# A clustered-attention, dense and routed-expert kernel: first pair's clusters and the passage to the dense layer in a new order, second products of 128-slot experts in rounded parts, 128 slots for the first expert

## The chip, the cores and the metric

One core of one Trainium2 chip runs the kernel. The metric is the device time of one execution in microseconds (us). Before the change three runs gave 716.62, 715.57 and 715.26 us, median 715.57.

## The reference, cut to what matters

Three layers follow each other: attention whose mask keeps a query and a key only if both chose the same of 16 centroids; a dense layer with an ELU between two products; and routed experts for the tokens whose skip score is positive.

```python
# attention: batch 2, heads 8, tokens 768, head size 64, 16 centroids per head
q_assign = argmax(einsum('bhsd,hcd->bhsc', q_n, c_n)); k_assign = argmax(einsum('bhsd,hcd->bhsc', k_n, c_n))
scores = where(q_assign == k_assign, (q @ k.T) / sqrt(D), -1e9)
x = softmax(scores) @ v                                # 1536 tokens x 512
# dense: w_in 512 x 2048, w_out 2048 x 512
h = x @ w_in;  g = where(h > 0, h, exp(min(h, 0)) - 1);  x = g @ w_out
# experts: 8 of them, w1 512 x 1024, w2 1024 x 512
xc = x[x @ w_skip > 0];  e_idx = argmax(xc @ w_gate);  gate = max of softmax(xc @ w_gate)
out[those] = xc + gate * (maximum(xc @ w1[e], 0) @ w2[e])      # e is the token's expert
```

## The kernel before, in words

**Attention.** The 16 (batch, head) blocks are done as 8 pairs of two heads. For a pair, q, k and v are loaded as `natq`, `natk`, `natv` (`load_nat`, L213). TensorE turns them (`turn`, L239) into PSUM; ACT rounds them to the high part `qH`, `kH` (`turn_head`, L247), and a subtraction gives the low part `qL`, `kL` (`turn_rest`: DVE for the first pair, POOL for the others, L259 and L261). Products of rounded values, three per product (high by high, low by high, high by low), then make the similarity to the centroids (`similar`, L280, 6 matmuls per 384 tokens). The clusters are chosen in a row of steps: turn back (L289), copy (L295), largest `mx` (L302), difference (L306), candidates (L311), first `mn` (L316), one-hot `oh` (L320), turn of the one-hot (L326), and the mask rows on ACT (L330). SP's queue moves q, k parts and mask rows into the operands `QA`, `KA`, `QB`, `KB` of each head (`move_qk`, `move_mask`). Then, in chunks of 128 queries: scores (L375), peak (L381, DVE), exponent (L388, ACT, tile `pe`), turning (flip, L397), high part `ptH` (L409, ACT), low part `ptL` (L415, DVE), product with the values (L428).

**Order.** Attention and the beginning of the dense layer are issued in an order written out by hand. `SCHEDULE` is a list of step names; `+` and `-` in front of a name mean the step of the next or the last pair. `attention` walks it once for each pair. Before the change the first `AHEAD = 20` steps of the second pair were issued ahead with the first pair's. In the last pair the names `W0` to `W6` stand for the dense layer's first products.

**Dense.** Weights are given in a form that is first rounded on the device to 32 bits of their own (`round_half`): ACT makes `cv_a` and `cv_t` (L644, L646), DVE makes `cv_a` again and `cv_b` in two steps (L648, L650, L653), POOL makes `r` (L655); ACT then takes `w1H` (L674) and POOL `w1L` (L675). The first two chunks' weights come from the generator `early_weights`, advanced by `next(self.early)` at places of the order and drained at the end of attention. `ffn_h` (L688) multiplies a chunk of 128 hidden columns for 384 tokens, 12 matmuls; `ffn_elu` is `e`, `e` on ACT, one DVE step into PSUM, `gH` on ACT, `gL` on DVE (L703 to L709); L720 is the second product. 32 rounds cover two halves of the tokens by 16 chunks.

**Experts.** Expert 0 is fixed as the first, the others are ranked by their count; each has so many slots as `WIDTHS` says (160, 160, 144, 128 five times). For the first expert the tokens of the second batch are picked by matmuls with a selection (`first_x`, L935), while a gathered tile gives those of the first batch. `expert` (L1086) runs 8 steps f of 128 hidden columns: first product of 4 matmuls (L1113), ReLU to `h` on ACT (L1115), second product one step later. With more than 128 slots ("not direct") the weights stand still and `h` moves, 4 matmuls per f with columns as wide as the slots (L1105), and the result `yT` is turned at the end (L1135). With 128 slots ("direct") `h` stands still and 512 columns of w2 move (L1102). All these are plain f32. `expert_load` fetches half an expert's w1 and w2, 1 MiB each, on SP's queue.

Of the kernel before, what the change touches and what calls it, by code (L numbers as in the profile page):

```python
# [27 lines left out]
WIDTHS = (160, 160, 144, 128, 128, 128, 128, 128)  # L28
# [10 lines left out]
AHEAD = 20  # L39
SCALE = {"q": 0.125, "k": 1.0}  # L40

LEAST_HI = struct.unpack("<f", struct.pack("<I", 897 << 20))[0]

# [17 lines left out]
class _Core:  # L61
# [24 lines left out]
    def centroids(self):  # L86
# [4 lines left out]
        nc.sync.dma_start(out=cn[:, 0, :], in_=self.cent.rearrange("h c d -> (h c) d"))  # L91
        self.load_nat(0, "qkv")
        self.zero = c.tile([128, 1], F32, name="zero")
        V.memset(self.zero, 0.0)
        S.activation(self.zero, self.zero, AF.Sqrt)
# [6 lines left out]
        t = c.tile([128, 8], F32, name="cnt")  # L102
# [4 lines left out]
        S.activation(self.zero, self.zero, AF.Exp)  # L107
# [105 lines left out]
    def load_nat(self, n, names):  # L213
        if n >= self.B * self.H // 2:
            return
        b, p = divmod(n, self.H // 2)
        for nm in names:
            src = {"q": self.q, "k": self.k, "v": self.v}[nm]
            shape = [128, 2, self.NC, 64] if nm == "v" else [128, self.NC, 2, 64]
            t = self.pre.tile(shape, F32, tag="nat" + nm, name="nat" + nm)  # L220
            for h in range(2):
                self.nc.sync.dma_start(out=t[:, h] if nm == "v" else t[:, :, h],
                                       in_=src[b, 2 * p + h].rearrange("(p c) d -> p c d", c=self.NC))
            self.nat[nm] = t
# [61 lines left out]
    def turn_back(self, n):  # L286
        ps = self.back[n] = self.bank_p()
        for c in range(self.NC):
            self.nc.tensor.transpose(ps[:, c * 64:c * 64 + 64], self.rows[0:64, c * 128:c * 128 + 128], self.ident[0:64, 0:64])  # L289

    def similarities(self, n):
        NG = self.NC * 4
        t = self.best[n] = {nm: self.pre.tile([128, NG] + [16] * w, dt, tag=nm, name=nm)
                            for nm, w, dt in (("eq", 1, F32), ("mx", 0, F32), ("mn", 0, F32), ("oh", 1, BF16))}
        self.nc.scalar.activation(t["eq"], self.back[n][:, 0:NG * 16].rearrange("p (g c) -> p g c", c=16), AF.Copy)  # L295

    def wide16(self, x):
        return x.unsqueeze(2).to_broadcast([128, self.NC * 4, 16])

    def largest(self, n):  # L300
        t = self.best[n]
        self.nc.vector.tensor_reduce(t["mx"], t["eq"], axis=AX.X, op=ALU.max)  # L302

    def less_largest(self, n):
        t = self.best[n]
        (self.nc.gpsimd if n else self.nc.vector).tensor_tensor(t["eq"], t["eq"], self.wide16(t["mx"]), ALU.subtract)  # L306

    def candidates(self, n):

        t = self.best[n]  # L310
        self.nc.vector.scalar_tensor_tensor(t["eq"], t["eq"], 0.0, self.iota_neg.unsqueeze(1).to_broadcast([128, self.NC * 4, 16]),  # L311
                                            ALU.is_equal, ALU.mult)

    def first_of_them(self, n):
        t = self.best[n]
        self.nc.vector.tensor_reduce(t["mn"], t["eq"], axis=AX.X, op=ALU.min)  # L316

    def one_hot(self, n):
        t = self.best[n]
        self.nc.vector.tensor_tensor(t["oh"], t["eq"], self.wide16(t["mn"]), ALU.is_equal)  # L320

    def turn_one_hot(self, n):
        oh, ps = self.best.pop(n)["oh"], self.bank_p()
        pb = self.rows_ps[n] = ps[0:64, :].bitcast(BF16)
        for c in range(self.NC):
            self.nc.tensor.transpose(pb[:, c * 128:c * 128 + 128],  # L326
                                     oh[:, 4 * c:4 * c + 4, :].rearrange("p g c -> p (g c)"), self.ident16)

    def mask_rows(self, n):
        self.nc.scalar.activation(self.rows[64:128].bitcast(F32R), self.rows_ps.pop(n)[:, 0:self.S], AF.Identity,  # L330
                                  scale=self.oh_sc[:, 0:1], bias=self.oh_sc[:, 1:2])

    def move(self, o, i):
        self.nc.sync.dma_start(out=o.bitcast(F32), in_=i.bitcast(F32))
# [13 lines left out]
    def move_mask(self, n, s):  # L348
        d, o = self.hd[s], self.rows[64:128]
        self.move(d["QB"][64:80], o[16 * s:16 * s + 16])  # L350
        self.move(d["KB"][64:80], o[32 + 16 * s:48 + 16 * s])
# [135 lines left out]
    def steps(self):  # L487
# [9 lines left out]
        for h in range(2):  # L497
            for nm in "qk":
                for x, f in (("turn", self.turn), ("TH", self.turn_head), ("raw", self.turn_raw), ("TL", self.turn_rest),
                             ("sim", self.similar)):  # L500
                    put(at, f"{x}{nm}{h}", f, nm, h)
            put(at, f"sT{h}", self.similar_out, h)
# [36 lines left out]
    def attention(self):  # L539
# [12 lines left out]
        order = []  # L552
        for m in range(-3, NPAIR + 3):
            for what in SCHEDULE:
                name = what.lstrip("+-")
                n = m + what.count("+") - what.count("-")
                if 0 <= n < NPAIR and name not in (end if n == NPAIR - 1 else last):
                    order.append((m, n, name))

        first = [x for x in order if x[1] == 1][:AHEAD]  # L560
        first = [x for x in order if x[0] < 0 or x in first]
        self.prep_tags = itertools.cycle(("p", "v", "t0", "t1"))
        for m, n, name in first:
            steps[name](n)
        self.prep_tags = itertools.repeat("p")
        for m, n, name in order:
            if (m, n, name) not in first:
                steps[name](n)
# [333 lines left out]
    def first_fetch(self):  # L902
# [9 lines left out]
        self.pick = d.tile([SLOT, 2, CAP], F32, name="pick")  # L912
        V.memset(self.pick, 0.0)
        self.early = []
        for g, n in enumerate((SLOT, CAP - SLOT)):
# [415 lines left out]
```

## Time and profile before

| what | value |
|---|---|
| median of 3 runs | 715.57 us (715.26 to 716.62) |
| profiled execution, its own time | 716.21 us |
| its span | 714.4 us |
| mean granted TensorE clock | 0.983 of full |
| busy share: PE, DVE, ACT, POOL | 95%, 62%, 59%, 38% |

The span is the time from the first to the last recorded instruction; 1.8 us of the profiled execution lie around it. A busy share is an average over stages. Attention takes the span up to about 259 us, the dense layer up to about 575 us with the routing in its tail, and the experts the rest. PE marks TensorE's matmuls, PEclk the share of full clock that it was granted.

### The profile page before, as it was taken

The page shows a single profiled execution, that of the slowest core. Times are in us where ns is not written, and L with a number is a line of the kernel's source. Part 1 is how long each engine was busy: PE and PEld are TensorE (multiplying, and loading weights), DVE is VectorE, ACT ScalarE, POOL GpSimd, SP SyncE. Part 2 cuts the span into 40 slices and gives each one's busy share as a digit, 9 for nine tenths or more (in the row PEclk, how much of TensorE's full clock was granted, in tenths as well). Part 3 has the DMA queues.
Part 4 walks back from the last instruction along what each step waited for, and adds up shares of the span by engine and source line. Part 5 has one row for each costly group of instructions (what it writes and reads, how often), then busy time and mean ns, then how long its engine had stood idle before and what let it go on. Part 6 is the DMA issues. An engine that isn't in the chain of part 4 may idle for free. (4 is left out here: it accounts for less than half of the span.)

```text
span 714.4 us, 12083 instructions
## 1 busy us (share of the span) xinstructions
PE 680.5 (95%) x4288; PEld 609.5 (85%) x4288; DVE 444.7 (62%) x836; ACT 422.3 (59%) x924; POOL 268.9 (38%) x257
## 2 busy tenths in 40 slices
PE   4899999999999987999999999999999999999994
PEld 3699999999999876888888899999998989987773
DVE  5499999999989987999999732522633521110100
ACT  4699989999898976677666655445444111111110
POOL 0423536444465043666888633322322032110010
PEclk9799999999999999999999999999999999999998
DMA  7646657366644613555555374151102278898830
GB/s 179 144 90 146 147 136 161 99 146 150 156 100 103 175 46 132 183 196 183 178 176 177 119 285 186 60 177 60 59 30 77 120 264 306 264 319 306 293 107 12
DMA packets 73829, 111.54 MB, mean 156 GB/s; under 512 B 31169, under 2 KB 41505, under 8 KB 73760
## 3 DMA queue, kind: packets, MB, share of 16 engines
q1 hardware_dynamic: 72176, 106.55, 50.5%
q0 software_dynamic: 1584, 4.13, 1.6%
q8 instruction: 36, 0.59, 0.4%
q14 instruction: 33, 0.27, 0.1%
HBM read 73.94 MB, written 16.99 MB: 127 GB/s over the span
## 5 line engine op out<-in xcount | busy, mean ns | idle before, releaser
L415 DVE TENSOR_TENSOR ptL<-ps_t,ptH 128x384 fp32r<-128x384 f32 x192 | 102.7, 551 | 12.2 <-ACT ptH L409 9.9
L409 ACT ACTIVATE ptH<-ps_t 128x384 fp32r<-128x384 f32 x192 | 91.4, 489 | 17.8 <-PE ps_t L397 13.7
L397 PE MATMUL ps_t<-ident,pe 128*128 128x128 f32 x576 | 94.4, 277 | 3.3 <-DVE ptL L415 2.6
L428 PE MATMUL ps_v<-ptH,vt 128*128 128x256 f32 x288 | 78.3, 296 | 0.7 <-DVE xr L445 0.7
L397 PEld LDWEIGHTS ps_t<-ident,pe 128*128 128x128 f32 x576 | 68.2, 141 | 11.7 <-DVE ptL L415 7.4
L428 PE MATMUL ps_v<-ptL,vt 128*128 128x256 f32 x288 | 77.1, 296 | 0.0
L675 POOL TENSOR_TENSOR w2L<-r,w2H 128x512 fp32r<-128x512 f32 x28 | 42.4, 1515 | 69.6 <-PE ps_t L720 62.3
L655 POOL TENSOR_TENSOR r<-cv_b,cv_t 128x512 int32<-128x512 int32 x32 | 43.1, 1346 | 46.3 <-DVE cv_b L653 26.4
L428 PEld LDWEIGHTS ps_v<-ptH,vt 128*128 128x128 f32 x288 | 54.0, 190 | 2.7 <-DVE xr L445 1.3
L428 PEld LDWEIGHTS ps_v<-ptL,vt 128*128 128x128 f32 x288 | 53.5, 190 | 0.0
L381 DVE TENSOR_REDUCE st<-ps_sA 128x1 f32<-128x768 f32 x48 | 45.6, 950 | 11.4 <-PE ps_sA L375 11.2
L1139 POOL DMA_INDIRECT out_dram<-o,dest x11 | 10.8, 980 | 105.2 <-DVE o L1137 104.3
L703 ACT ACTIVATE e<-ps_p 128x384 f32<-128x384 f32 x32 | 15.7, 490 | 58.6 <-PE ps_p L688 58.6
L648 DVE SCALAR_TENSOR_TENSOR cv_a<-cv_a,d 128x512 f32<-128x512 f32 x32 | 45.6, 1425 | 5.4 <-ACT cv_a L644 5.1
L381 DVE TENSOR_REDUCE st<-ps_sB 128x1 f32<-128x768 f32 x48 | 45.7, 952 | 2.8 <-PE ps_sB L375 2.7
L688 PE MATMUL ps_p<-xH,w1H 128*128 128x384 f32 x128 | 44.0, 344 | 3.1 <-ACT w1H L674 3.1
L675 POOL TENSOR_TENSOR w1L<-r,w1H 128x512 fp32r<-128x512 f32 x32 | 44.1, 1379 | 7.1 <-ACT w1H L674 7.1
L388 ACT ACTIVATE pe<-ps_sA,st 128x768 f32<-128x768 f32 x48 | 43.4, 904 | 0.1
L706 DVE SCALAR_TENSOR_TENSOR ps_p<-e,ps_p 128x384 f32<-128x384 f32 x32 | 17.9, 559 | 40.9 <-ACT e L704 40.9
L388 ACT ACTIVATE pe<-ps_sB,st 128x768 f32<-128x768 f32 x48 | 43.0, 896 | 0.5 <-DVE st L381 0.3
L688 PE MATMUL ps_p<-xL,w1H 128*128 128x384 f32 x128 | 43.1, 336 | 0.0
L1115 ACT ACTIVATE h<-ps_v 128x128 f32<-128x128 f32 (+2 forms) x32 | 9.1, 285 | 56.1 <-PE ps_v L1113 47.1
(362 smaller groups left out, 1883.0 us busy)
## 6 DMA issues: line engine op xcount, KB each, us to landing
ew<-in_moe_w_dram SPq DMA_DIRECT2D x32, 1024.0 KB
d<-in_moe_w_in_dram SPq DMA_DIRECT2D x16, 512.0 KB
d<-in_moe_w_out_dram SPq DMA_DIRECT2D x16, 512.0 KB
wf_d<-r SPq DMA_DIRECT2D x16, 512.0 KB
r<-wf_d SPq DMA_DIRECT2D x16, 512.0 KB
KA<-kH SPq DMA_DIRECT2D x32, 192.0 KB
natq<-in_q_dram SPq DMA_DIRECT2D x16, 192.0 KB
natk<-in_k_dram SPq DMA_DIRECT2D x16, 192.0 KB
```

The lines of the kernel that those rows point to most:

```text
L381: self.nc.vector.tensor_reduce(st, self.sc[u][:, :, 0:384], axis=AX.XY, op=ALU.max, negate=True)
L388: self.nc.scalar.activation(pe, self.sc.pop(u)[:, :, 0:384], AF.Exp, bias=self.peaks.pop(u), accum_out=self.sums[n][:, s:s + 1])
L397: self.nc.tensor.transpose(ps[:, 0, j * 128:j * 128 + 128], self.pe[u][:, half, j * 128:j * 128 + 128], self.ident)
L409: self.nc.scalar.activation(self.split(u, half)[0], self.tp[u, half][:, 0, 0:384].rearrange("p (c q) -> p c q", c=3), AF.Copy)
L415: self.nc.vector.tensor_tensor(l, self.tp.pop((u, half))[:, 0, 0:384].rearrange("p (c q) -> p c q", c=3), h.bitcast(F32), ALU.subtract)
L428: self.nc.tensor.matmul(self.vp[n, j], lhsT=self.vt[n][:, j // NG, c, :], rhs=t, start=(part == 0 and i == 0), stop=(part == 3 and i == 2 ...
L648: V.scalar_tensor_tensor(a, a, LEAST_HI, hi.bitcast(F32), ALU.is_ge, ALU.mult)
L655: G.tensor_tensor(out.bitcast(I32), b, t, ALU.add)
L675: self.nc.gpsimd.tensor_tensor(l, x, h.bitcast(F32), ALU.subtract)
L688: self.nc.tensor.matmul(ps, lhsT=w[:, c, :], rhs=x[:, c, :], start=(i == 0), stop=(i == 11))
L703: S.activation(e, ps, AF.Relu, scale=-1.0)
L706: V.scalar_tensor_tensor(ps, e, -1.0, ps, ALU.add, ALU.max)
```

## The change

It has four parts.

- **Start.** The first pair's q is loaded first, centroids and k from ACT's queue, v from SP's. A list `START` replaces `AHEAD`. The first pair's choice of clusters is made in two halves of 192 columns, read straight from PSUM, without ACT's copy; half of the masks of keys moves on ACT's queue; scores of the first pair are issued before the second pair's similarities.
- **Passage.** The generator of early weights has five single steps for the first chunk, and `W0` to `W3` (`first_h`) each advance it once more.
- **First expert.** `WIDTHS[0]` is 128, not 160: it becomes a direct expert, and its selection matmuls have 128 columns and one group.
- **Second products of 128-slot experts.** `h` and w2 are split into rounded high and low parts (`hH`, `hL`; `ew2H`, `ew2L` or both in `ew2HL`), and three products of rounded values replace the f32 product. ACT makes the high parts, DVE the low ones, w2's two steps f ahead (`w2_split`).

```diff
-WIDTHS = (160, 160, 144, 128, 128, 128, 128, 128)
+WIDTHS = (128, 160, 144, 128, 128, 128, 128, 128)
...
+START = """
+    turnq0 THq0 turnq1 TLq0 THq1 turnk0 TLq1 THk0 turnk1 TLk0 THk1 TLk1 simq0 simk0 loadqk sT0 simq1 simk1 back0 mx0 sT1
...
-        nc.sync.dma_start(out=cn[:, 0, :], in_=self.cent.rearrange("h c d -> (h c) d"))
-        self.load_nat(0, "qkv")
...
+        self.load_nat(0, "q")
+        nc.scalar.dma_start(out=cn[:, 0, :], in_=self.cent.rearrange("h c d -> (h c) d"))
+        self.load_nat(0, "k", nc.scalar)
+        self.load_nat(0, "v")
...
+    def largest(self, n, half=None):
+        t, g = self.best[n], self.groups_of(half)
+        self.nc.vector.tensor_reduce(t["mx"][:, g], (t["eq"] if n else self.back_groups(n))[:, g], axis=AX.X, op=ALU.max)
...
+        self.move(d["KB"][64:80], o[32 + 16 * s:48 + 16 * s], None if n or s else self.nc.scalar)
...
-            put(last, f"W{i}", lambda n, i: self.ffn_h(0, 0, 3 * i, 3 * i + 3), i)
+            put(last, f"W{i}", self.first_h, i)
...
+    def first_h(self, n, i):
+
+        self.ffn_h(0, 0, 3 * i, 3 * i + 3)
+        next(self.early, None)
...
-            for n in (2, 1, 1, 1):
+            for n in ((2, 1, 1, 1) if k else (1, 1, 1, 1, 1)):
...
+    def w2_split(self, e, f):
+
+        if e == self.E or WIDTHS[e] > SLOT:
+            return
+        j, i = divmod(f, self.F2 // 256)
+        w2 = self.ew[e, j][1][:, i, :]
+
+        if f % 2:
+            h, l = (self.fw.tile([128, 512], F32R, tag="w1" + x, bufs=2, name="ew2" + x) for x in "HL")
+        else:
+            hl = self.fw.tile([128, 2, 512], F32R, tag="r", bufs=3, name="ew2HL")
+            h, l = hl[:, 0], hl[:, 1]
+        self.nc.scalar.activation(h, w2, AF.Copy)
+        self.nc.vector.tensor_tensor(l, w2, h.bitcast(F32), ALU.subtract)
+        self.e2[e, f] = h, l
...
-                PE.matmul(y[0][0:W], lhsT=h, rhs=w2, start=(f == 0), stop=(f == NF - 1))
+                (hH, hL), (wH, wL) = h, w2
+                for i, (a, b) in enumerate(((hH, wH), (hL, wH), (hH, wL))):
+                    PE.matmul(y[0][0:W], lhsT=a, rhs=b, start=(f == 0 and i == 0), stop=(f == NF - 1 and i == 2))
...
-            S.activation(h, ps[:, 0:W], AF.Relu)
+            if direct:
+                hH, hL = h = [d.tile([128, SLOT], F32R, tag="h" + x, bufs=3, name="h" + x)[:, 0:W] for x in "HL"]
+                S.activation(hH, ps[:, 0:W], AF.Relu)
+                V.scalar_tensor_tensor(hL, ps[:, 0:W], 0.0, hH.bitcast(F32), ALU.max, ALU.subtract)
```

TensorE's order at the start, from the last of the second pair's turned keys (`natk`) on. Before, the second pair's similarities (`qH` to `kL` by the centroid weights `cwH`, `cwL`) come ahead of the first scores (`KA`, `QA`):

```order
L239 MATMUL ps_t_298<-ident,natk 128x128 x3
L280 MATMUL ps_p<-qH,cwH 64x384
L280 MATMUL ps_p<-qL,cwH 64x384
L280 MATMUL ps_p<-qH,cwL 64x384
L280 MATMUL ps_p<-kH,cwH 64x384
L280 MATMUL ps_p<-kL,cwH 64x384
L280 MATMUL ps_p<-kH,cwL 64x384
L375 MATMUL ps_sA<-KA_76,QA_75 128x384
L375 MATMUL ps_sA<-KB_78,QB_77 128x384
```

After the change the same place reads:

```order
L244 MATMUL ps_t_299<-ident,natk 128x128 x3
L401 MATMUL ps_sA<-KA_76,QA_75 128x384
L401 MATMUL ps_sA<-KB_78,QB_77 128x384
...
L423 MATMUL ps_t_334<-ident,pe 128x128 x3
L285 MATMUL ps_p<-qH,cwH 64x384
L285 MATMUL ps_p<-qL,cwH 64x384
L285 MATMUL ps_p<-qH,cwL 64x384
L285 MATMUL ps_p<-kH,cwH 64x384
```

Three chunks of scores (12 matmuls) and the first flip of `pe` now stand between the second pair's turned keys and its similarities.

ACT's order at the passage to the dense layer, before, from the first chunk's `w1H` on. `cv_a` and `cv_t` begin the rounding of the second chunk, and the second `w1H` ends it; `e` and `gH` are the first ELU:

```order
L674 ACTIVATE w1H<-r 128x512
L409 ACTIVATE ptH<-ps_t_4026 128x3x128
L388 ACTIVATE pe,sums<-ps_sA,st 128x768
L644 ACTIVATE cv_a<-d_3686 128x512
L646 ACTIVATE cv_t<-d_3686 128x512
...
L409 ACTIVATE ptH<-ps_t_4119 128x3x128
L703 ACTIVATE e<-ps_p 128x384
L704 ACTIVATE e<-e 128x384
L707 ACTIVATE gH<-ps_p 128x384
L437 ACTIVATE xtmp<-ps_v 64x256
L674 ACTIVATE w1H<-r 128x512
```

And with the change:

```order
L705 ACTIVATE w1H<-r 128x512
L435 ACTIVATE ptH<-ps_t_4039 128x3x128
L463 ACTIVATE xtmp<-ps_v 64x256
L435 ACTIVATE ptH<-ps_t_4056 128x3x128
L414 ACTIVATE pe,sums<-ps_sB,st 128x768
L675 ACTIVATE cv_a<-d_3688 128x512
L677 ACTIVATE cv_t<-d_3688 128x512
...
L435 ACTIVATE ptH<-ps_t_4122 128x3x128
L705 ACTIVATE w1H<-r 128x512
L734 ACTIVATE e<-ps_p 128x384
L735 ACTIVATE e<-e 128x384
```

`cv_a` and `cv_t` moved behind the last exponent (`pe` from `ps_sB`), and the second `w1H` stands ahead of the first ELU, no longer behind it.

TensorE's order in the last expert, a 128-slot one, before; `xs,ew` is the first product, `ew,h` the second:

```order
L1113 MATMUL ps_p<-xs,ew_7977 128x128 x4
L1102 MATMUL ps_t_8063<-ew_7978,h 128x512
L1113 MATMUL ps_v<-xs,ew_7977 128x128 x4
L1102 MATMUL ps_t_8063<-ew_7978,h 128x512 x2
```

With the change:

```order
L1166 MATMUL ps_v<-xs,ew_8170 128x128 x4
L1151 MATMUL ps_t_8316<-ew2HL,hH 128x512
L1151 MATMUL ps_t_8316<-ew2HL,hL 128x512
L1151 MATMUL ps_t_8316<-ew2HL,hH 128x512
L1151 MATMUL ps_t_8316<-ew2H,hH 128x512
L1151 MATMUL ps_t_8316<-ew2H,hL 128x512
L1151 MATMUL ps_t_8316<-ew2L,hH 128x512
```

One f32 instruction per step became three on rounded parts; the same rows now also stand for the first expert.

## Rows read from the trace of the kernel before

**Rows 1.** Granted TensorE clock in the page's 40 equal slices, in tenths of full speed

```profile
PEclk9799999999999999999999999999999999999998
```

**Rows 2.** Stretches: length; busy us (x) of PE, PEld, DVE, ACT, POOL; PEclk, DMA share, GB/s

```profile
0.00:18.00 18.00, 8.37 (x40) 6.24 (x41) 9.14 (x41) 8.26 (x14) 1.40 (x10) 0.90 0.79 178
72.00:250.00 178.00, 176.58 (x1330) 164.55 (x1328) 165.17 (x284) 162.89 (x370) 79.62 (x93) 1.00 0.59 137
580.00:590.00 10.00, 8.76 (x65) 8.52 (x64) 0.00 (x0) 1.10 (x4) 3.74 (x4) 1.00 1.04 362
640.00:660.00 20.00, 20.00 (x111) 14.02 (x110) 1.44 (x2) 3.05 (x11) 2.08 (x3) 1.00 0.90 312
```

**Rows 3.** Timeline of SP's queue and PE at the start: begin, duration, work, wait

```profile
1.28 1.37 SPq L222 DMA_DIRECT2D natq<-in_q_dram  x2
...
5.85 0.87 PE L239 MATMUL ps_p<-ident,natq 128*128 128x128 f32 x3 [5.85 <-DMA natq<-in_q_dram]
...
24.27 0.34 PE L375 MATMUL ps_sA<-KA,QA 128*128 128x384 f32 x1
```

**Rows 4.** Timeline of ACT and of DVE in the choice of clusters, pair 0

```profile
17.61 0.99 ACT L330 ACTIVATE rows<-ps_t,oh_sc 64x768 fp32r<-64x768 bf16 x1 [3.89 <-PE ps_t L326]
...
13.75 0.55 DVE L302 TENSOR_REDUCE mx<-eq 128x24 f32<-128x384 f32 x1 [3.58 <-ACT eq L295]
```

**Rows 5.** Stretch behind the passage, columns as in rows 2

```profile
275.00:280.00 5.00, 3.96 (x16) 3.97 (x17) 3.16 (x5) 3.86 (x9) 1.90 (x3) 0.73 0.20 63
```

**Rows 6.** Timeline at the passage: PE, DVE and POOL

```profile
276.04 0.44 PE L688 MATMUL ps_p<-xH,w1H 128*128 128x384 f32 x1 [3.09 <-ACT w1H L674]
...
272.24 0.56 DVE L709 TENSOR_TENSOR gL<-ps_p,gH 128x384 fp32r<-128x384 f32 x1
...
273.17 0.75 DVE L653 SCALAR_TENSOR_TENSOR cv_b<-cv_a,top,cv_b 128x512 int32<-128x512 int32 x1
...
274.06 1.26 POOL L655 TENSOR_TENSOR r<-cv_b,cv_t 128x512 int32<-128x512 int32 x1 [8.43 <-DVE cv_b L653]
```

**Rows 7.** Timeline of PE in the routing tail, second selection group to next work

```profile
560.54 0.63 PE L935 MATMUL ps_sA<-pick,xg 32*128 32x32 f32 x4
...
561.54 0.66 PE L845 MATMUL ps_p<-ident,xL 128*128 128x128 f32 x4
```

**Rows 8.** Timeline of PE in the first expert

```profile
586.35 0.81 PE L1105 MATMUL ps_sA<-h,ew 128*128 128x160 f32 x4 [1.24 <-ACT h L1115]
...
589.72 1.25 PE L1113 MATMUL ps_p<-xs,ew 128*128 128x160 f32 x8
...
591.89 0.71 PE L1113 MATMUL ps_v<-xs,ew 128*128 128x160 f32 x4
...
599.40 0.60 PE L1135 MATMUL ps_t<-ident,yT 128*128 128x128 f32 x4
599.84 0.44 PE L1105 MATMUL ps_sA<-h,ew 128*128 128x160 f32 x2
```

**Rows 9.** Timeline of PE in a 128-slot expert, and in dense rounds of rounded parts

```profile
643.78 1.05 PE L1113 MATMUL ps_p<-xs,ew 128*128 128x128 f32 x8
644.67 1.02 PE L1102 MATMUL ps_t<-ew,h 128*128 128x512 f32 x2
645.53 1.05 PE L1113 MATMUL ps_v<-xs,ew 128*128 128x128 f32 x8
...
325.78 0.39 PE L720 MATMUL ps_sA<-w2H,gL 128*128 128x512 f32 x1
326.01 0.39 PE L720 MATMUL ps_sA<-w2H,gH 128*128 128x512 f32 x1
```

**Rows 10.** Groups by line and shape: busy us, mean ns, idle ahead of them

```profile
L674 ACT ACTIVATE w1H<-r 128x512 fp32r<-128x512 f32 x32 | 19.8, 619 | 7.9 <-DMA r<-wf_d 4.3 <-POOL r L655 3.6
...
L1137 DVE SCALAR_TENSOR_TENSOR o<-ps_t,by_rank,xg 128x512 f32<-128x512 f32 x8 | 6.0, 750 | 36.9 <-PE ps_t L1102 31.4 <-PE ps_t L1135 5.5
L1115 ACT ACTIVATE h<-ps_p 128x128 f32<-128x128 f32 x20 | 5.5, 277 | 28.7 <-PE ps_p L1113 28.1 <-PE ps_t L1102 0.6
```

More of the change, by code (lines that the diff above doesn't have):

```diff
@@ L284, in similar_out, with turn_back @@
         self.nc.scalar.activation(self.rows[0:64, half * 384:half * 384 + 384], self.sim.pop((n, half))[0:64, 0:384], AF.Copy)
[L286 to L289, printed above, removed]
+    def turn_back(self, n, half=None):
+        if not half:
+            self.back[n] = self.bank_p()
+        for c in self.chunks(half):
+            self.nc.tensor.transpose(self.back[n][:, c * 64:c * 64 + 64], self.rows[0:64, c * 128:c * 128 + 128],
+                                     self.ident[0:64, 0:64])
+        if not half:
+            NG = self.NC * 4
+            self.best[n] = {nm: self.pre.tile([128, NG] + [16] * w, dt, tag=nm, name=nm)
+                            for nm, w, dt in (("eq", 1, F32), ("mx", 0, F32), ("mn", 0, F32), ("oh", 1, BF16))}
@@ L291, in similarities, with chunks, back_groups, groups_of @@
+    def chunks(self, half):
+        HC = self.NC // 2
+        return range(self.NC) if half is None else range(half * HC, half * HC + HC)
+    def back_groups(self, n):
+        NG = self.NC * 4
+        return self.back[n][:, 0:NG * 16].rearrange("p (g c) -> p g c", c=16)
+    def groups_of(self, half):
+        c = self.chunks(half)
+        return slice(4 * c[0], 4 * c[-1] + 4)
     def similarities(self, n):
[L292 to L294 removed]
@@ L501, in steps @@
                     put(at, f"{x}{nm}{h}", f, nm, h)
+            for name, f in (("back", self.turn_back), ("mx", self.largest), ("eqsub", self.less_largest),
+                            ("first", self.candidates), ("least", self.first_of_them), ("equal", self.one_hot),
+                            ("rows", self.turn_one_hot), ("oT", self.mask_rows)):
+                put(at, f"{name}{h}", f, h)
             put(at, f"sT{h}", self.similar_out, h)
@@ L551, in attention @@
         steps = at | end | last
-        order = []
-        for m in range(-3, NPAIR + 3):
+        self.prep_tags = itertools.cycle(("p", "v", "t0", "t1"))
+        done = set()
+        for what in START:
+            name, n = what.lstrip("+"), what.count("+")
+            steps[name](n)
+            done.add((n, name))
+        self.prep_tags = itertools.repeat("p")
+        for m in range(NPAIR + 3):
             for what in SCHEDULE:
@@ L556, in attention @@
                 n = m + what.count("+") - what.count("-")
[L557 to L568, printed above, removed]
+                if 0 <= n < NPAIR and name not in (end if n == NPAIR - 1 else last) and (n, name) not in done:
+                    steps[name](n)
         self.drain(self.early)
@@ L1287, in run @@
             self.expert_load()
+        self.e2 = {}
+        for f in range(2):
+            self.w2_split(0, f)
         for e in range(E):
```

104 lines of the change are left out of this document (55 added, 49 removed).

## The prediction

> **What bounds the kernel now.** I read the granted clock first, then busy time by stretch, then the timelines of the places that the change touches. The clock row says that TensorE ran at full speed except in the second slice [rows 1]; a gain must come from less work or fewer waits. By stretch, PE is busy 176.58 of 178 us in the body of attention and 20.00 of 20 in the late experts; in the first 18 us it is busy for 8.37 [rows 2]. So three kinds of time are to be had: PE's idle time at the start, that at the passage to the dense layer, and PE's own work in the experts, where every us off a product counts. DVE and ACT are nearly idle in the experts: 1.44 and 3.05 of 20 us [rows 2].
>
> The sum is made against the profiled execution, 716.2 us; the median of the runs is 715.6, so the forecast may stand 0.6 high.
>
> **Start: -5.2 us.** PE waits 5.85 us for q and begins with scores only at 24.27 [rows 3]. The first pair's mask rows are made by 17.61 + 0.99 = 18.6, after ACT waited 3.89 us for the turned one-hot [rows 4]; then they need a transfer into the operands. Up to 24.27 PE turns and compares the second pair, for which nothing of the first waits. With those similarities behind the first scores, scores begin when the mask has landed. The choice in halves overlaps DVE, PE and ACT: one DVE step takes 0.55 us for 384 columns [rows 4], so five take 2.8 in one piece; with 192 columns each the second half follows the first through PE and ACT, ACT's copy ahead of the first step (about one DVE step) goes, and ACT's last piece is half of 0.99. Together I put the last mask row 2 us sooner, at 16.6. Its landing no row shows. The nearest is q, issued at 1.28 and in use at 5.85, 4.6 us for loads of four times the size [rows 3]; between 0 and 4.6 I take 1.7, as the piece is small. First scores at 18.3, 6.0 sooner, less about 0.8 for the second pair's six similarities that now stand among the scores: -5.2. Bounds: with 4.6 for the landing 21.2, so -3.1 and with the similarities -2.3; with the similarities in bubbles and a quicker landing -6.5.
>
> Loading k and centroids from ACT's queue I cost at nothing. The stretch has a DMA share of 0.79 while it moves 178 GB/s [rows 2]: the transfers, not the issues, fill it. The Trainium skill ("DMA: Bandwidth & Descriptors", Issuing engines are not separate DMA queues) says the same for any kernel: issues from several engines interleave on the same 16 DMA engines and save issue time alone; by it q's landing stays about where it is, and nothing of the sum hangs on that.
>
> **Passage: -1.9 us.** PE waits 3.09 us for the second chunk's `w1H` at 276.04 [rows 6], and the clock then falls: 0.73 of full over 275 to 280 [rows 5], 0.27 x 5 = 1.35 us lost. The chain is DVE `cv_b`, done at 273.17 + 0.75, POOL `r` at 274.06 + 1.26, then ACT `w1H` [rows 6]. With the change DVE's two `cv_b` steps and POOL's `r` come before the ELU, so `w1H` is ready some 4 us sooner. What is late next is the bank `ps_p` of the first ELU: the new product writes it, and its last reader `gL` now ends at 272.24 + 0.56 [rows 6]. That chain becomes later, since `w1H` now stands on ACT ahead of `e`, and waits there for POOL's `r`; `gH` and the part of the output behind it on ACT wait too, and DVE's steps behind them. By hand I get the next product at 274.9 instead of 276.04, and DVE, whose chain paces the dense rounds after that, 1.9 us ahead since its two `cv_b` steps now lie in its waits. Bounds: 0, if the added wait on ACT eats the gain; -4.4, if both the idle 3.09 and the 1.35 of the clock go. I take -1.9, since a gap of about 2 us stays.
>
> **Routing tail: -2.0 us.** The second selection group lasts 1.0 us, 560.54 to 561.54 [rows 7], and goes. Seven further steps of eight matmuls have 128 columns in place of 160. The price of one such f32 record at 160 is 2.17/16 = 0.136 us (589.72 to 591.89 [rows 8]), at 128 it is 0.89/8 = 0.111 (643.78 to 644.67 [rows 9]): 7 x 8 x 0.025 = 1.4. PE is the bound here; -2.4 in full, -1.0 if the narrower columns gain nothing; -2.0.
>
> **First expert: -5.7 us.** One step f costs 2.17 us now [rows 8]. As a 128-slot one it has a first product of 0.89 [rows 9] and three products of rounded parts, each 512 columns. The dense layer runs just that shape at a spacing of 0.23 us (325.78 to 326.01, to the rows' hundredth [rows 9]), which I put at 0.225: 0.675. Eight steps: 8 x (2.17 - 1.565) = -4.84. The turns of `yT`, four per group of tokens at 0.44 (599.40 to 599.84 [rows 8]), two groups, go too: -0.9; the wait of 1.24 us for `h` at 586.35 [rows 8] may go or stay. Against it, the turns of the second expert's tokens come behind all products of the first now, and then wait for a copy to SBUF, +0.5. Bounds -4.0 (the wait comes back, and the bubble is 1.5) and -7.2 (the wait is gone as well). I take -5.7: 4.84 and 0.9 sure, the bubble's 0.5 against half of the wait.
>
> **Experts 3 to 7: -7.4 us.** The f32 second product takes 0.86 us per step (644.67 to 645.53 [rows 9]), its replacement 0.675: 5 x 8 x 0.185 = -7.4. The added work is ACT's 128x512 copy, 0.62 as `w1H`, beside the ReLU's 0.28, and DVE's 128x512 subtraction, 0.75 by the DVE row of that size, beside a 128x128 one, which I take at 0.3 (that size on ACT) [rows 10]. So ACT has 0.9 us and DVE about 1.05 per step of 1.565 us. Both fit, and the splits are two steps ahead. The five splits of the first expert move into the dense layer's last rounds, where they lie beside PE. If this cover fails, a step costs what DVE or ACT need; the first rival prices that. At the end one 128x128 subtraction comes ahead of the last products: +0.2.
>
> **Sum.** -5.2 - 1.9 - 2.0 - 5.7 - 7.4 + 0.2 = -22.0; 716.2 - 22.0 = 694.2, so **694 us**.
>
> **The rivals.**
> - *Experts go to the pace of transfers.* A 128-slot expert takes 8 x 1.75 = 14.0 us in the trace with a DMA share of 0.90 and 312 GB/s [rows 2]. At 8 x 1.565 = 12.5 us it would ask for 312 x 14.0 / 12.5 = 349 GB/s; the most that a row shows is 362, at a share of 1.04 [rows 2]. Also ACT must not wait for a load, since ReLUs are queued behind its split. If loads or splits hold each such expert at about 13.4 us, five give back 4.5: 699 us. For it: the share has little room. Against: loads run ahead by four buffers, and the last expert's come early.
> - *The passage is cured whole.* If `w1H`, the ELU and the bank all come early enough, the 1.35 us of the low clock go too and the whole 3.09: 4.4 in place of 1.9, 691.7 us. Against: the wait that is new on ACT.
> - *The start gains little.* If the early scores only run into the next wait (DVE's or ACT's part of the first chunks, or masks that land late), 5.2 becomes 0 to 1: 699 us. For it: the transfers fill 0.79 of the first 18 us [rows 2], so masks may land late. Against: in attention's body PE is the busiest engine, at 176.58 of 178 us [rows 2].
> - *Slower: the clock falls in the experts.* Where PE waits, the clock can fall: after the 3.09 us wait it was 0.73 [rows 6, 5]. If the three products wait in every step f, for the low parts of DVE or for ACT's splits behind a load, TensorE may stay at 1.2 GHz through six experts, about 75 us. At half clock work takes twice its time: from 22 us of such work on, a third of the stage, the gain of 22 is used up, and with all of it 694 + 75 = 769 us. Against it: waits in the first expert of 1.24 us [rows 8] left the clock at 1.00 [rows 2]. The Trainium skill ("TensorE: Matmul & The Clock Gate", HAM oscillation) describes a loop whose every round waits for a load and is throttled each time; by it this would be likely only if the loads bound the loop, and no row here shows that.
> - *It doesn't do what it says.* More than 128 tokens of the first expert would go through the overflow loop; the inputs give it 49, so this is left out.
>
> **How the numbers follow.** Forecast 0.52, transfers or splits 0.20, passage cured 0.12, start without gain 0.11, slower 0.05, of which 0.01 is the case where the low clock just eats the gain. All good ends together, -6.5 - 4.4 - 2.4 - 7.2 - 7.4, give -27.9, 688; the low ends together -2.3 - 0 - 1 - 4 - 2.9 = -10.2, 706 (for experts 3 to 7 the 7.4 less the 4.5 of the first rival). Ends do not all meet, and two rivals at a time are rare, so the range is 687.5 to 702. A measurement tells about 0.2%, 1.4 us: faster 0.94 (the forecast and three rivals, less 0.01 for the unseen), same 0.02, slower 0.04.
>
> **What would show it.** In the changed profile: PE's first scores at 18 to 19; a wait of some 2 us ahead of the second chunk's first product, with a dip of the clock; no 160-column rows of the first expert and steps of 1.56 us in it; in experts 3 to 7 steps of 1.56 us with PE busy throughout, DVE and ACT at some 60% and DMA near 350 GB/s. It is wrong if the steps stay near 1.75 with PE waiting, if PEclk falls in the experts, or if the first scores begin after 21.

## The result, and the profile after

The changed kernel takes 698.56 us (median of 4 runs, 697.12 to 700.11) against 715.55 us before; the ratio is 0.9758, 95% interval 0.9735 to 0.9782. It is faster by 17 us; the forecast was 694, with a range of 687.5 to 702. The profiled execution took 699.52 us, its span is 697.8. Two later groups of five runs gave the ratios 0.9746 (0.9729 to 0.9763) and 0.9763 (0.9742 to 0.9783).

The time goes as follows between places that both programs have, read from TensorE's timeline (us; a place is where its first instruction begins, but the last product with values is taken at its end; "again" is the changed kernel profiled a second time):

| from | before | after | again | forecast of the change |
|---|---|---|---|---|
| 0 to the first product with values | 37.08 | 37.17 | 37.27 | -5.2 |
| to the last product with values | 233.67 | 233.37 | 233.13 | 0 |
| to the first second product of the dense layer | 11.33 | 9.17 | 9.18 | -1.9 with the next row |
| to the first selection matmul | 277.28 | 276.88 | 276.87 | |
| to the first product of the experts | 16.13 | 15.66 | 14.03 | -2.0 |
| to the end of PE | 129.74 | 116.58 | 116.59 | -12.9 |
| to the end of the span | 9.17 | 8.97 | | |

So the experts gave 13.2 us where 12.9 were forecast, the passage with the dense layer 2.6, the routing tail 0.5 or 2.1, and the start nothing. The measured time is the 699 us that the rival "the start gains little" gave. Some 1.5 of the experts' 13.2 us are a stall that the profile before shows and these two do not; the section on the prediction says how that is read.

The stretches of the changed kernel that answer to [rows 2, 5], with one in the routing tail; columns as there:

```profile
0.00:18.00 18.00, 9.09 (x40) 6.68 (x40) 9.61 (x44) 7.44 (x13) 3.27 (x13) 0.98 0.79 174
72.00:250.00 178.00, 176.84 (x1335) 165.30 (x1334) 166.05 (x285) 162.71 (x370) 79.41 (x93) 1.00 0.59 138
275.00:280.00 5.00, 4.45 (x25) 4.13 (x25) 4.75 (x8) 4.26 (x9) 1.30 (x2) 1.00 0.58 160
565.00:575.00 10.00, 9.37 (x72) 8.80 (x71) 6.47 (x50) 1.09 (x5) 0.82 (x1) 0.83 0.47 175
580.00:590.00 10.00, 9.53 (x68) 8.53 (x67) 3.21 (x7) 2.42 (x8) 3.22 (x4) 1.00 1.04 369
640.00:660.00 20.00, 20.00 (x142) 18.43 (x141) 12.49 (x27) 11.22 (x25) 2.06 (x2) 1.00 0.97 345
```

In the experts PE is still busy 20.00 of 20 us, now with DVE at 12.49 and ACT at 11.22, some 60% each, and the transfers at 345 GB/s with a share of 0.97. The clock is 1.00 in both stretches of the experts shown.

TensorE's timeline of the changed kernel at the start, which answers to [rows 3]:

```profile
5.89 0.87 PE L244 MATMUL ps_p<-ident,natq 128*128 128x128 f32 x3 [5.89 <-DMA natq<-in_q_dram]
...
8.03 0.48 PE L122 MATMUL ps_sA<-ident,cn 128*128 128x128 f32 x1 [0.63 <-DVE cn L120]
...
13.11 0.53 PE L285 MATMUL ps_v<-kH,cwL 128*64 128x384 f32 x1
...
20.34 0.67 PE L401 MATMUL ps_sA<-KA,QA 128*128 128x384 f32 x1
23.03 0.66 PE L401 MATMUL ps_sA<-KB,QB 80*128 80x384 f32 x1 [2.02 <-DMA KB<-rows]
...
28.34 0.67 PE L285 MATMUL ps_p<-qH,cwH 128*64 128x384 f32 x1
...
30.41 0.52 PE L401 MATMUL ps_sB<-KA,QA 128*128 128x384 f32 x1
```

The last similarity of the first pair begins at 13.11. Before, it was at

```profile
11.89 0.33 PE L280 MATMUL ps_v<-kH,cwL 128*64 128x384 f32 x1
```

ACT's, DVE's and the queue's rows of the changed kernel, which answer to [rows 4]:

```profile
17.22 0.67 ACT L356 ACTIVATE rows<-ps_v,oh_sc 64x384 fp32r<-64x384 bf16 x1 [0.84 <-PE ps_v L350]
19.26 0.67 ACT L356 ACTIVATE rows<-ps_v,oh_sc 64x384 fp32r<-64x384 bf16 x1 [1.37 <-PE ps_v L350]
19.95 0.62 ACTq L360 DMA_DIRECT2D KB<-rows  x1
...
7.32 0.56 DVE L266 SCALAR_TENSOR_TENSOR qL<-ps_p,qH 128x384 fp32r<-128x384 f32 x1 [1.77 <-ACT qH L252]
7.79 0.18 DVE L120 COPY cn<-cn 128x64 f32<-128x64 f32 x1
...
14.12 0.36 DVE L323 TENSOR_REDUCE mx<-ps_t 128x12 f32<-128x192 f32 x1 [3.21 <-PE ps_t L296]
...
18.28 0.36 DVE L343 TENSOR_TENSOR oh<-eq,mn 128x192 bf16<-128x192 f32 x1
```

The product of scores that holds the masks waits for their transfer: the last mask row is made at 19.93, 1.3 us later than before, and is in use at 23.03. The first product of scores begins at 20.34, but it holds no masks, and its partner stands still until 23.03; the prediction gave a begin after 21 as a sign of being wrong. The similarities of the second pair then take 2.07 us (28.34 to 30.41) among the scores.

The choice of clusters itself, from the begin of the last similarity to the end of the last mask row, takes 6.82 us (13.11 to 19.93) against 6.71 before (11.89 to 18.60). So the masks are late because the similarities are, and the new choice wins nothing back.

The passage (PE, ACT, DVE, POOL), against [rows 6]; behind the wait of 1.99 us the clock stays at 1.00 (275 to 280 above), where the prediction expected a dip:

```profile
274.75 0.41 PE L719 MATMUL ps_p<-xH,w1H 128*128 128x384 f32 x1 [1.99 <-DVE gL L740]
...
270.49 0.63 ACT L705 ACTIVATE w1H<-r 128x512 fp32r<-128x512 f32 x1 [2.20 <-POOL r L686]
271.03 0.47 ACT L734 ACTIVATE e<-ps_p 128x384 f32<-128x384 f32 x1
...
274.05 0.56 DVE L740 TENSOR_TENSOR gL<-ps_p,gH 128x384 fp32r<-128x384 f32 x1
...
269.18 1.28 POOL L686 TENSOR_TENSOR r<-cv_b,cv_t 128x512 int32<-128x512 int32 x1 [6.03 <-DVE cv_b L684]
```

And one step of a 128-slot expert, against [rows 9]:

```profile
640.00 1.05 PE L1166 MATMUL ps_p<-xs,ew 128*128 128x128 f32 x8
640.80 0.47 PE L1151 MATMUL ps_t<-ew2H,hH 128*128 128x512 f32 x1
641.12 0.39 PE L1151 MATMUL ps_t<-ew2H,hL 128*128 128x512 f32 x1
641.35 0.39 PE L1151 MATMUL ps_t<-ew2L,hH 128*128 128x512 f32 x1
641.58 1.05 PE L1166 MATMUL ps_v<-xs,ew 128*128 128x128 f32 x8
```

The step takes 1.58 us (640.00 to 641.58) against 1.75 before. The first of the three products begins 0.32 ahead of the second, not 0.23, while the four matmuls of the first product now take 0.80 (640.00 to 640.80) and not 0.89.

### The profile page after: what moved, and what is told of

Its sections match the earlier page's. It is cut to its first block, busy times and chain, and to the rows that moved or that the text cites. A ratio compares the mean times of both kernels' runs of the same rounds, so it can differ in the third digit from the quotient of the medians.

```text
span 697.8 us, 12196 instructions
## 1 busy us (share of the span) xinstructions
PE 666.6 (96%) x4272; PEld 608.7 (87%) x4272; DVE 487.2 (70%) x933; ACT 446.7 (64%) x968; POOL 268.3 (38%) x254
## 5 line engine op out<-in xcount | busy, mean ns | idle before, releaser
L719 PE MATMUL ps_v<-xL,w1H 128*128 128x384 f32 x124 | 41.4, 334 | 0.0
```

Of the source, the lines that this page charges most:

```text
L719: self.nc.tensor.matmul(ps, lhsT=w[:, c, :], rhs=x[:, c, :], start=(i == 0), stop=(i == 11))
```

## The experiments

Three groups of four kernels, each timed in five rounds beside the kernel before. The first and the third hold the changed kernel itself as their measure; the second does not, so its kernels are compared with the changed kernel by their ratios to the kernel before. Where a difference is read from profiles, it is one execution against another.

### The changed kernel again

No edit.

> The changed kernel once more, as the measure for the other runs. Theory: the time is 697 to 700 us, and the 3 us between its runs come from the clock's dip in the routing tail, there or not there. If that is so, the profile shows PEclk 1.00 around 566 to 570 us in a run near 697 and about 0.6 in one near 699.5. Rival: the dip is always there and the spread comes from elsewhere, then a run near 697 shows it too.

Measured: 697.73 us (696.59 to 699.06). The stretch of the routing tail in this profile:

```profile
565.00:575.00 10.00, 9.37 (x83) 8.67 (x82) 6.83 (x50) 1.83 (x7) 1.99 (x3) 1.00 0.50 172
```

The dip of the clock that cost the first profile 1.6 us (0.83 in 565 to 575, tail 15.66 against 14.03) is not there, and the time of this execution is 1.8 us less. With it away, the tail gains 2.1 us. The program is the same: the dip is a matter of the single execution. It is not all of the scatter: a stall in the first expert, told of at the end, is another part. All later profiles but that of the kernel with 160 slots, whose tail is longer, show the tail at 14.03 or 14.04.

### The start as before

```diff
+AHEAD = 20
...
-        for what in START:
-            name, n = what.lstrip("+"), what.count("+")
-            steps[name](n)
-            done.add((n, name))
+        for m, n, name in first:
+            steps[name](n)
```

The loads' queues, the choice of clusters in one piece after ACT's copy, and the masks on SP's queue are as before, too.

> The changed kernel with the whole start as before (loads, order, choice of clusters in one piece). Theory, from the two traces: the new start is worth nothing, since in the body of attention both traces are level to 0.2 us; then this runs within 0.5 us of the changed kernel. Rival, as predicted: the start is worth 5.2 us and something later ate it; then this is 3 to 5 us slower.

Measured: 697.86 us, 0.1 us from the changed kernel of the group. The first product with values is at 37.49. So the whole new start gains nothing. How far one profile can be trusted here is seen from the seven that share the new start unaltered: their first product with values is at 35.84 to 37.72.

### The passage as before

```diff
-            put(last, f"W{i}", self.first_h, i)
+            put(last, f"W{i}", lambda n, i: self.ffn_h(0, 0, 3 * i, 3 * i + 3), i)
...
-            for n in ((2, 1, 1, 1) if k else (1, 1, 1, 1, 1)):
+            for n in (2, 1, 1, 1):
```

> The changed kernel with the passage as before. Theory, from the two traces: the passage is worth 3.4 us, so this is 3 to 3.5 us slower than the changed kernel, with the wait of 3.1 us and the low clock behind it. Rival, as predicted: 1.9 us slower.

Measured: 699.95 us, 2.2 us slower, and the old wait is back:

```profile
274.77 0.69 PE L714 MATMUL ps_p<-xH,w1H 128*128 128x384 f32 x1 [3.07 <-ACT w1H L700]
```

From the last product with values to the first selection matmul it takes 11.29 + 276.90 = 288.19 us, the changed kernel 9.17 + 276.88 = 286.05. So the passage is worth 2.1 us by this pair, nearer to the 1.9 of the prediction than to the 3.4 that I had read from the two traces at first: the expectation missed, and its rival held.

### Plain second products

```diff
...
-                (hH, hL), (wH, wL) = h, w2
-                for i, (a, b) in enumerate(((hH, wH), (hL, wH), (hH, wL))):
-                    PE.matmul(y[0][0:W], lhsT=a, rhs=b, start=(f == 0 and i == 0), stop=(f == NF - 1 and i == 2))
+                PE.matmul(y[0][0:W], lhsT=h, rhs=w2, start=(f == 0), stop=(f == NF - 1))
...
```

The splits themselves go, too.

> The changed kernel with plain f32 second products for the 128-slot experts, the first one of them. Predicted: six experts of 8 steps at 1.75 in place of 1.565 us, 8.9 us slower less the 0.2 of the end. By the steps of 1.58 that the changed kernel's trace shows it is 48 x 0.17 = 8.1 us slower. Rival: the DMA paces the experts either way, then 4 us or less.

Measured: 705.28 us, 7.6 us slower than the group's changed kernel. The 48 steps are worth 0.16 us each. Experts 3 to 7 take 73.83 us, as in the kernel before, and 67.16 in the changed kernel. Transfers do not pace the experts: PE waits 0.4 us for `h` of the first expert with plain products, and 0.4 us for `hH` with rounded parts.

### The choice in one piece

```diff
...
-    back1 eqsub0 first0 +turnq0 least0 +rawq0 equal0 +THq0 +turnq1 rows0 +TLq0 mx1 eqsub1 +rawq1 first1 oT0 least1 +THq1
+    back mx +turnq0 eqsub +rawq0 first +THq0 least +turnq1 equal +TLq0 rows +rawq1 oT +THq1 +TLq1
...
```

> The changed kernel with the first pair's choice of clusters in one piece, still read straight from PSUM and still with the scores ahead of the second pair's similarities. Theory: the halves are what makes the masks late, ten DVE steps of 0.36 us and more in place of five of 0.56; here the last mask row is made 0.5 to 1 us sooner than the 19.9 of the changed kernel, the first masked score comes as much sooner than 23.0, and the time is 0.5 to 1 us less. Rival, as predicted: halves overlap the engines, so this is about 1 us slower.

Measured: 697.74 us, ratio 0.9749 (0.9730 to 0.9769), no difference. The last similarity and the last mask row are

```profile
13.71 0.34 PE L285 MATMUL ps_v<-kH,cwL 128*64 128x384 f32 x1
...
19.21 0.99 ACT L356 ACTIVATE rows<-ps_v,oh_sc 64x768 fp32r<-64x768 bf16 x1 [2.81 <-PE ps_v L350]
```

The row is there at 20.20, 6.49 us behind the begin of that similarity. In halves it is 6.82 us in the first profile and 6.34 to 6.81 in the six others with that start. So these rows show neither gain nor loss by the halves. My theory here fell, and so did the 1 us of the prediction. That the ten DVE steps of some 0.36 in place of five of some 0.55 eat what the overlap brings fits this, but is argued.

### The first loads on SP's queue

```diff
...
-        self.load_nat(0, "q")
-        nc.scalar.dma_start(out=cn[:, 0, :], in_=self.cent.rearrange("h c d -> (h c) d"))
-        self.load_nat(0, "k", nc.scalar)
-        self.load_nat(0, "v")
+        nc.sync.dma_start(out=cn[:, 0, :], in_=self.cent.rearrange("h c d -> (h c) d"))
+        self.load_nat(0, "qkv")
+        self.zero = c.tile([128, 1], F32, name="zero")
+        V.memset(self.zero, 0.0)
+        S.activation(self.zero, self.zero, AF.Sqrt)
...
-        S.activation(t[:, 8:9], t[:, 1:2], AF.Exp, scale=0.0)
...
+        S.activation(self.zero, self.zero, AF.Exp)
...
```

Two things go back at once: the queues, and ACT's first steps on a tile `zero`, which the change had dropped together with them.

> The changed kernel with the first loads as before, all on SP with the centroids first. Theory: in the changed kernel DVE takes the copy of the centroids only behind a low part of q, TensorE waits 0.63 us for it at 8.0 us and makes the first similarities at a spacing of 0.32 us up to 13.1; here that wait goes, the similarities end about 1 us sooner, the masks with them, and the time is about 1 us less. Rival: with k behind q and v the loads are later, or the masks meet another wait, then no difference.

Measured: 695.73 us (695.31 to 696.36), ratio 0.9732 (0.9716 to 0.9749), and the first product with values at 35.63 in place of 37.2. PE, and then DVE:

```profile
8.78 0.55 PE L285 MATMUL ps_p<-qH,cwH 128*64 128x384 f32 x1
9.13 0.52 PE L285 MATMUL ps_p<-qL,cwH 128*64 128x384 f32 x1
...
9.77 0.37 PE L285 MATMUL ps_p<-kH,cwH 128*64 128x384 f32 x1
9.98 0.34 PE L285 MATMUL ps_p<-kL,cwH 128*64 128x384 f32 x1
...
20.69 0.66 PE L401 MATMUL ps_sA<-KB,QB 80*128 80x384 f32 x1 [2.00 <-DMA KB<-rows]
...
6.82 0.20 DVE L120 COPY cn<-cn 128x64 f32<-128x64 f32 x1
7.03 0.56 DVE L266 SCALAR_TENSOR_TENSOR qL<-ps_p,qH 128x384 fp32r<-128x384 f32 x1
```

The wait of 0.63 us for the copy of the centroids is gone: DVE takes the copy ahead of `qL`, not behind it. In the changed kernel the scaled centroids are there at 5.55 already, but DVE waits 1.77 us for `qH` with the copy queued behind `qL` (7.32 and 7.79 above). The similarities run at a spacing of some 0.2 us from 9.77 on; in the changed kernel they stay at 0.32 to the end. The masks are in use 2.3 us sooner.

So this part of the start, which the prediction costed at nothing, costs something, by the order that DVE's steps take. How much is less sure. The masks are in use at 20.4 to 21.1 in the three profiles with this edit and at 22.2 to 23.6 in the nine with the changed loads; the first product with values is at 35.63 here, inside the 35.84 to 37.72 of the unaltered start but for 0.2 us, and the intervals of the ratios overlap. Which of the two things that went back sets DVE's order was not separated. It is not the transfers of q: q is in use at 5.89 after, 5.85 before [rows 3]. That agrees with the Trainium skill ("DMA: Bandwidth & Descriptors", Issuing engines are not separate DMA queues), which says that issuing from several engines saves issue time alone.

### Similarities in the gap of the masks

```diff
-    equal1 rows1 +TLq1 oT1 moveT0 moveO0 +turnk0 +rawk0 +THk0 moveT1 +turnk1 +TLk0 +rawk1 +THk1 +TLk1
+    equal1 rows1 +TLq1 oT1 moveT0 moveO0 +turnk0 +rawk0 +THk0 moveT1 +turnk1 +simq0 +TLk0 +rawk1 +THk1 +TLk1
```

> The changed kernel with the three matmuls of the second pair's first query similarities moved into the gap of 2 us in which TensorE waits for the masks. Theory: that gap is the transfer of the mask rows and nothing depends on what fills it, so about 1 us of matmuls at the low clock comes off what stands behind the scores: 0.5 to 1 us less. Rival: the clock or DVE's peak bounds the stretch behind, then no difference.

Measured: 696.38 us (695.39 to 697.92), ratio 0.9742 (0.9723 to 0.9761). The gap shrinks as meant:

```profile
23.42 0.66 PE L401 MATMUL ps_sA<-KB,QB 80*128 80x384 f32 x1 [1.04 <-DMA KB<-rows]
```

The first product with values comes at 36.89, 0.3 us sooner than in the first two profiles of the changed kernel. That is within what the same start scatters (35.84 to 37.72), and so is the time, so no gain is shown.

### 160 slots for the first expert

```diff
-WIDTHS = (128, 160, 144, 128, 128, 128, 128, 128)
+WIDTHS = (160, 160, 144, 128, 128, 128, 128, 128)
...
```

> The changed kernel with 160 slots for the first expert, the rounded parts for experts 3 to 7 alone. Predicted for the width: 5.7 us in the expert and 2.0 in the routing tail, so this is 7.7 us slower. By the traces 6.5 and 2: about 8.3 us slower, without what the clock's dip adds. Rival: the gain of the expert is given back by transfers, then 5 us or less.

Measured: 707.12 us, ratio 0.9889 (0.9870 to 0.9908), some 10 us slower than the changed kernel by the ratios. The tail is 16.14 us as before, 2.1 more. The first two experts take 37.31 us (573.19 to 610.50) against 32.32 in the changed kernel (572.25 to 604.57), 5.0 more. The rest holds more than the width: the third expert, the same in both, takes 21.92 us against 17.10.

```profile
612.09 0.63 ACT L1129 ACTIVATE ew2HL<-ew 128x512 fp32r<-128x512 f32 x1 [4.29 <-DMA ew<-in_moe_w_dram]
...
614.52 0.90 PE L1154 MATMUL ps_sA<-h,ew 128*128 128x160 f32 x4 [2.88 <-ACT h L1173]
...
610.00:620.00 10.00, 7.12 (x43) 6.88 (x43) 2.99 (x5) 3.56 (x9) 0.00 (x0) 0.83 0.71 214
```

The last two lines are PE's timeline and a stretch. ACT's splits of the fourth expert's weights stand ahead of the second expert's last ReLU; their load has not landed, ACT waits 4.29 us with the ReLU queued behind, PE waits 2.88 us, and the clock is at 0.83 over the 10 us. That is the first rival's mechanism, and it is real; in the changed kernel's profile no split waits for a load. The transfers are not at their limit there, at a share of 0.71: the wait is one of order.

### The changed kernel a third time

No edit.

> The changed kernel as the measure of this group: 697 to 698.5 us, with the wait of 2.0 us for the bank of the first ELU at the passage.

Measured: 700.11 us (699.03 to 700.17), ratio 0.9763, above the range that I expected. The passage shows the same 2.00 us; a wait of 0.99 us for `hH` in the first expert is new, and that expert takes 16.59 us in place of 14.96; more on it at the end.

### The high part behind the ELU's first steps

```diff
             next(g, None)
-            self.w_split(k, 0)
             if k == 0:
+                self.w_split(k, 0)
                 yield
...
-        for i in range(4, 7):
+        put(last, "W4", self.first_elu)
+        for i in range(5, 7):
...
+    def first_elu(self, n):
+        next(self.elu[0])
+        self.w_split(1, 0)
```

> The changed kernel with the second chunk's high part on ACT behind the two steps e of the first ELU instead of ahead of them. Theory: in the changed kernel that high part waits 2.2 us for POOL's r, with e queued behind, so the bank of the first ELU comes free 1.7 us later than it could, and the wait of 2.0 us at the passage is this; here the wait is below 0.5 us, the clock does not fall behind it, and the time is 1.5 to 2.5 us less. Rival: DVE bounds the first dense rounds, so the 2 us are lost again within the next rounds and the time is the same.

Measured: 698.66 us (696.26 to 699.87), 1.4 us less than the group's changed kernel, ratio 0.9742 (0.9717 to 0.9768), which overlaps the changed kernel's (0.9742 to 0.9783).

```profile
272.81 0.41 PE L724 MATMUL ps_p<-xH,w1H 128*128 128x384 f32 x1 [0.33 <-DVE gL L745]
278.33 0.50 PE L756 MATMUL ps_sA<-w2H,gH 128*128 128x512 f32 x1 [1.11 <-ACT w2H L710]
```

The wait of 2.0 us is 0.33, so the added wait on ACT was its cause. The next wait, for `w2H`, grows from 0.5 to 1.1 and gives a part back: from the last product with values to the first selection matmul 8.08 + 276.89 = 284.97, 1.1 us less than the changed kernel. By the profiles this is clear: up to the dense layer's first second product it is 8.06 to 8.08 us in the three with this edit, and 9.15 to 9.18 in the seven others that have the 2.0 us wait without a dip of the clock. Half of the theory's gain holds, the other half goes to the rival: the chain behind that next wait is DVE `cv_b`, POOL `r`, ACT `w2H`, and `cv_b` ends only 1.4 us sooner (275.83, in the changed kernel 277.21).

### Loads and high part together, and all three

The edits of `loads_sp` and `w1h_after_e`, and those with that of `fill_gap`. These two kernels are `both` and `all_three`.

> That order and the first loads on SP together. Theory: the two lie in stages that wait for nothing of each other, so the gains add: 1.6 and 1.5 to 2.5 us, 693.5 to 695 us. Rival: one of the two eats the other, then 695.5 us as with the loads alone.

> Both, and the second pair's first query similarities in the gap of the masks. Theory: 0.5 us less than both. Rival: with the masks sooner the gap closes before the low part of the second pair's q is there, TensorE waits for POOL, and it is the same or slower.

Measured: 697.28 us (ratio 0.9734, 0.9713 to 0.9755) and 696.02 us (695.20 to 697.58; ratio 0.9710, 0.9690 to 0.9729), in a group where the changed kernel took 700.11. All three is 4.1 us faster than the changed kernel of its group, and the intervals of these two ratios lie apart; against the changed kernel's other groups (0.9746 and 0.9758) it is some 2.6 to 3.4 us by the ratios. The first kernel missed the 693.5 to 695 us expected and by its ratio is no better than the loads alone (0.9732). The places show why: the start and the passage keep their gains (first product with values at 35.98 and 34.43, passage 8.06 and 8.08), but the first expert takes 18.77 and 18.79 us in place of 14.96 and takes 3.8 us back. Here the kernel with both edits, with a stretch behind the wait:

```profile
579.08 0.51 PE L1156 MATMUL ps_t<-ew2HL,hH 128*128 128x512 f32 x1 [1.70 <-ACT hH L1174]
...
578.75 0.28 ACT L1174 ACTIVATE hH<-ps_p 128x128 fp32r<-128x128 f32 x1 [3.36 <-PE ps_v L1171]
...
580.00:585.00 5.00, 5.00 (x24) 4.43 (x23) 1.06 (x4) 0.56 (x2) 0.00 (x0) 0.66 1.04 375
```

So a wait of 1.7 us is followed by 5 us at a clock of 0.66, another 1.7 us. In `all_three` the wait is 1.87 us, and the clock is 0.83 over 575 to 585.

## Why the prediction was right, and where it was not

- **Experts: right in mechanism, with luck in the numbers.** -5.7 - 7.4 + 0.2 = -12.9 forecast, -13.2 measured. By timeline experts 3 to 7 gave 6.7 us, forecast 7.2 with the end. The step is 1.58 us where 1.565 was forecast, by two misses that cancel: the three products need 0.78 and not 0.675, since the first one begins 0.32 ahead of the second, while the first product takes 0.80 and not 0.89. The first two experts gave 6.5 us, forecast 5.7, but some 1.5 of them are the stall of the kernel before. The kernel with 160 slots shows the old first two experts without that stall, 37.31 us in place of 38.81, and against them the change gives 5.0 us. The prediction counted half of that wait as a gain; in the first two profiles it is away, in the third a like one is back (0.99 us). The bubble ahead of the second expert is as forecast: PE waits 0.47 us for `xs`, forecast 0.5. DVE and ACT hid the splits (60% busy, at 0.71 and 0.63 us per 128x512 split, forecast 0.75 and 0.62):

```profile
L1130 DVE TENSOR_TENSOR ew2L<-ew,ew2H 128x512 fp32r<-128x512 f32 x24 | 17.1, 713 | 7.4 <-ACT ew2H L1129 7.3
...
L1129 ACT ACTIVATE ew2H<-ew 128x512 fp32r<-128x512 f32 x24 | 15.1, 629 | 4.9 <-PE ps_t L1151 4.2 <-PE ps_v L719 0.6
```

- **Passage: right in mechanism, 0.2 to 0.7 short.** The wait for `ps_p` behind `gL` is where it was forecast (274.75; forecast 274.9), with 1.99 us (some 2), and -2.1 to -2.6 stands against -1.9. The dip of the clock that it expected behind that wait comes in two of the nine profiles with that wait (0.66 over 275 to 280 with the start as before and with plain products), and it costs nothing. With the same instructions there, the part up to the dense layer's first second product is 9.17 us without the dip and 10.04 (start as before) or 10.02 (plain products) with it, and the dense part that follows is 276.88, 276.06 and 276.02: the sums are 286.05, 286.10 and 286.04. DVE takes the difference back: its `gL` of the second chunk begins at 282.43 in the first profile, without the dip, and at 282.40 with the start as before, with it. So the rival that wanted 2.5 us more from this place could not have had the 1.35 of the clock.
- **Routing tail: right (2.1 of 2.0)**, but for the dip of the clock in one of the profiles.
- **Start: wrong.** The step that failed is "Together I put the last mask row 2 us sooner, at 16.6". It is made at 19.93, 1.3 us later than before. The choice in halves and without ACT's copy takes as long as the old one (6.82 us, before 6.71), and the similarities ahead of it are late (the last one begins at 13.11, before at 11.89: the wait of 0.63 us for the centroids, and a spacing that stays at 0.32). That wait goes with the change of the loads, which the prediction costed at nothing, or with that of ACT's first steps, which neither it nor the list of changes names. Two more terms were too good: the landing took 3.1 us from issue to use (19.95 to 23.03; 3.0 to 3.1 in eleven other profiles), not 1.7, and the similarities among the scores 2.07 us at a clock of 0.50, not 0.8. The landing would have told it ahead: before, the masks were ready at 18.6, and with 3.1 us for the landing they could be in use at 21.7, while scores began at 24.27 [rows 3]. So with the masks where they were, the order could give 2.6 us at most, an estimate, and the moved similarities cost 2.07 of them: some half a us was left, unless the masks came sooner. The rival "the start gains little" (699 us, chance 0.11) is what came to pass, by late masks. It gives the measured total, too.
- **The other rivals.** The low clock in the experts did not come in the changed kernel: PE's longest waits there are 0.37 and 0.47 us, and the clock is 1.00 over 575 to 680. But single falls are real: behind one wait of 1.7 to 1.9 us in two of the later kernels (0.66 over 5 us, 0.83 over 10), and behind 2.88 us in the kernel with 160 slots (0.83 over 10 us). Each cost under 2 us and none came again in the rounds behind it. The Trainium skill ("TensorE: Matmul & The Clock Gate", HAM oscillation) describes a loop with a wait in every round, and no run here has one. Transfers at 345 GB/s and a share of 0.97 are near the 362 of before, yet in the changed kernel nothing waited for them.
- **The clock row.** "Full speed except in the second slice" was read too simply: a 9 there stands for 90% or more, so it hides short dips, as the 0.73 of [rows 5], and the last slice is an 8.

## What to carry to other kernels

Work that stands ahead of a critical step may be filling the latency of a transfer: before moving it, take the time from the step's last input to its use, and count as gain only what is left over after the moved work has been paid where it goes. Changing how the first loads are issued can change the order in which another engine takes its steps, so look at that engine's order, not only at transfer times. A split of operands into rounded parts pays where, as here, the engines that make the parts are idle, but each split queues ahead of the steps that the bound engine waits for, so it must not be placed before its load has landed. And before a stage's gain is taken from one profile, compare the same stage in several: here the same program differed by 1.6 us in its tail and by as much in its first expert.

## What was not expected of the hardware

- **A DVE step of half the width is not half as long.** 0.36 us for 128x192 against 0.55 for 128x384 [rows 4]: halving five steps costs 5 x (2 x 0.36 - 0.55) = 0.85 us of DVE.
- **The clock at the very start.** The windows give PEclk 1.00 up to about 14 us, but 384 columns have a spacing of 0.32 us there, as from 24 to 30 us, where the clock is 0.50 (1.2 GHz); at 1.00 later on it is 0.18. The faster spacing comes between 8.8 and 10.9 us in the five profiles in which TensorE worked without a break from its first turn on. In the nine in which it had waited 0.63 us for the centroids it comes at 11.9, 13.2 and 13.5 in three and behind the similarities in six. So that wait goes with a second loss, whose size differs between executions of the same start.
- **A stall in the first expert.** In the kernel before and in all four of the last group, but in none of the other nine profiles, ACT starts a ReLU late, and PE waits 1 to 1.9 us for it (1.24 before [rows 8]), at a DMA share of 1.03 to 1.05, which the profiles without the stall show as well. The releaser that the trace names had long been done. The first expert then takes 16.59 to 18.79 us in place of 14.96, the most where the clock falls behind the wait. What ACT waits for there was not settled, and no run was made for it.
